# Attention ahead of two expert layers: its pieces in a listed order instead of a planned one

## The chip, the cores and the metric

The kernel runs on one core of one Trainium2 chip. The metric is the device time of one execution in microseconds (us), as the median of several executions. Engines are named as in the profile: PE (TensorE, matrix products), PEld (its loading of weights, which overlaps PE), DVE (VectorE), ACT (ScalarE), POOL (GpSimd) and SP (SyncE, which here issues DMA transfers). PSUM, where PE writes its products, has eight banks.

## What is computed

Attention in fp32 with 4 batches, 12 heads, 448 positions and head size 64, in which the heads are mixed before and after the softmax, and then two gated layers on the 1792 tokens of width 768:

```python
scores = scale * np.matmul(q, k.transpose(0, 1, 3, 2))
scores = np.einsum('bhij,hg->bgij', scores, w_pre)
scores = scores - np.max(scores, axis=-1, keepdims=True)
attn = np.exp(scores)
attn = attn / (np.sum(attn, axis=-1, keepdims=True) + 1e-09)
attn = np.einsum('bhij,hg->bgij', attn, w_post)
return np.matmul(attn, v)
...
x = (1 / (1 + np.exp(-(x @ w_gate))) * (x @ w_val)) @ w_out      # 768 -> 1536 -> 768
h = x @ w_in                                                      # 768 -> 2048
return (h * (1.0 / (1.0 + np.exp(-1.702 * h)))) @ w_out2          # -> 768
```

## The kernel before

The kernel first does the attention (function `attention`, L128) and then the layers (class `Ffn`). This change is about the attention, about 400 of 1308 us, and about the point at which one hands over to the other.

Each batch has four units of rows (three of 120, one of 88), 16 units in all, and each unit is cut into groups of rows that fill the 128 partitions with all heads, 92 groups `s` in all. PE's work comes in five kinds of pieces, called by a letter from here on:

- **T**, `turn` (L269): four transposes of q or k (some pieces have two), into one bank; ACT or DVE copies the high part out, DVE makes the low part.
- **S**, `qk` (L309): the scores of one pair of heads of one unit, six matmuls into two banks; two copies to `sc` by ACT or DVE (`qk_out`).
- **P**, `premix` (L337): the heads' first mixing for one group, from a tile `gt` that two DMAs (`relayout`, L328, issued by SP) fill out of `sc`. There are five `gt` tiles: group s can be moved when P of group s-5 is done. P writes two banks; then DVE takes the maxima (L343), ACT the exponentials (L349), ACT, DVE and POOL make the scaled second mixing matrix (L357, L359, L362).
- **O**, `postmix` (L384): the second mixing of the group, 56 short matmuls in the trace, into two banks; two copies to `at` by ACT or DVE (`post_out`).
- **A**, `av` (L405): the product with v for one unit, in two halves. Each half has three thirds of 16 matmuls, which write one bank.

T, S, P and O, and A divide PE's array in different ways ("rows", "quad" and "columns" in the code).

The order of all pieces on all engines is made by a planner when the kernel is built. `Work.add` (L37) takes a piece with its due time, its cost on each engine that can do it, what it needs, what buffers and how many banks it takes. `Work.order` (L60) then again and again takes the piece that can start first by these costs, picks its engine and its banks, and reckons a delay in PE's supply of instructions (`fetched`, L48, with blocks of 256). Every engine then does its pieces in that order, one behind the other; semaphores keep the dependences.

`add_scores` (L474) makes a piece of two pairs of heads for all units but the first, where it is one pair. `add_av` (L526) makes one piece of a whole half (`AVS` has one entry of three thirds), so an A piece is 48 matmuls. Beside this, `prepare` (L890) converts 28 blocks of the layers' weights during the attention, and `begin` (L794) adds the first steps of the layers: loads of x, the conversion of four blocks of weights, and 12 first pieces of matmuls (`early`, L831; written `pg` in the trace, six matmuls each). In these four blocks the storing of a converted block to memory (L869, by SP) belongs to the piece `conv3` on DVE, so it stands in SP's queue where `conv3` stands in the order.

Of the kernel before, what the change touches and what calls it, by code (L numbers as in the profile page):

```python
# [20 lines left out]
class Work:  # L21
# [20 lines left out]
                                load=load, lead=lead))  # L42
        return self.pieces[-1]

    def room(self, x):
        return sorted((t, b) for b, t in self.open.items() if b < self.kept or not x["late"])[:x["wants"]]

    def fetched(self, x, start):  # L48

        busy, late = x["engines"]["PE"]  # L50
        at, left, n = start, x["size"], self.room_in
        since = self.since
        while left > n:
            at += busy * n / x["size"]
            left -= n
            at = since = max(at, since + FETCH)
            n = BLOCK
        return at + busy * left / max(x["size"], 1) - start - busy, n - left, since

    def order(self):  # L60
        now = {}
        self.room_in, self.since = FIRST_BLOCK, -FETCH
        self.loaded = 0.0
        mode = None
        open_ = sorted(self.pieces, key=lambda x: (x["due"], x["i"]))
        done = []
        while open_:
            best = None
            for x in open_[:AHEAD] + open_[-FILL:]:
                if any(n["end"] is None for n in x["needs"] + x["behind"]):  # L70
                    continue
                at = max([n["end"] - x["lead"] for n in x["needs"]] + [n["begin"] for n in x["behind"]] + [x["since"]])
                wants = {p: x["takes"].count(p) for p in x["takes"]}
                if any(len(self.free[p]) < c for p, c in wants.items()):
                    continue
                at = max([at] + [sorted(self.free[p])[c - 1] for p, c in wants.items()])
                if x["wants"]:
                    room = self.room(x)
                    if len(room) < x["wants"]:
                        continue  # L80
                    at = max(at, room[-1][0])
                for e, (busy, _) in x["engines"].items():
                    start = max(at, now.get(e, 0.0))
                    key = (start + (self.fetched(x, start)[0] if x["size"] else 0.0), x["due"], x["i"])
                    if best is None or key < best[0]:
                        best = (key, x, e)
            _, x, e = best
            start = max([n["end"] - x["lead"] for n in x["needs"]] + [n["begin"] for n in x["behind"]] + [x["since"], now.get(e, 0.0)] +
                        [sorted(self.free[p])[x["takes"].count(p) - 1] for p in x["takes"]] + [t for t, _ in self.room(x)])
            busy, late = x["engines"][e]  # L90
            if e == "PE" and x["mode"] != mode:
                start += self.modes[mode == "quad"]
                mode = x["mode"]
            if x["size"]:
                wait, self.room_in, self.since = self.fetched(x, start)
                busy, late = busy + wait, late + wait
            if x["load"]:
                self.loaded = max(self.loaded, start + ISSUE) + x["load"]
                late += self.loaded - start
            for p in x["takes"]:  # L100
                self.free[p].remove(min(self.free[p]))
            x["banks"] = [b for _, b in self.room(x)]
            for b in x["banks"]:
                del self.open[b]
            x["begin"] = start
            x["end"] = start + late
            now[e] = start + busy
            for p in x["gives"]:
                self.free[p].append(x["end"])
            for y, n in x["frees"]:  # L110
                self.open[y["banks"][n]] = x["end"]
            open_.remove(x)
            done.append((start, x["i"], x, e))
        self.span = max(x["end"] for x in self.pieces)
        done.sort(key=lambda y: y[:2])
        return [(x, e) for _, _, x, e in done]


AHEAD = 400
BLOCK = 256  # L120
FIRST_BLOCK = 193
FETCH = 4090
ISSUE = 1451
END = 1e9
FILL = 140


def attention(tc, q, k, v, w_pre, w_post, xd, after):  # L128
# [8 lines left out]
    B, H, S, D = q.shape  # L137
    NP = H // 2
# [18 lines left out]
    for b in range(B):  # L157
        i0 = 0
# [22 lines left out]
    with ExitStack() as ctx:  # L181
# [243 lines left out]
        build_w()  # L425

        STEP = 3581
        AVS = ((0, 1, 2),)
        AVH = 3824
        AVR = 0  # L430
        TAIL = first[len(units) - 1]
# [94 lines left out]
        def add_av(u):  # L526
            b, i0, n = units[u]
            t = (first[u] + last[u] + 2) * STEP + -5918
            late = first[u] + last[u] + 1 >= TAIL
            prev = []  # L530
            x = None
            for half in range(2):
                for some in AVS:
                    done = half == 1 and some is AVS[-1]
                    y = work.add(t + half * AVH + some[0] * AVR, dict(PE=(21 * n - len(some) + 3, 21 * n + 180)),
                                 lambda e, half=half, some=some: av(u, half, some), needs=[] if x else out[u] + [vready[b, c] for c in range(2)],
                                 behind=[x] if x else [], banks=0 if some[0] else 1, late=late, mode="columns", size=32 * len(some),
                                 gives=() if not done else ("a", "v") if u % nu == nu - 1 else ("a",))
                    x = y
                    if some[0] == 0:  # L540
                        holds = x
                prev = [work.add(t + half * AVH + 2410, dict(ACT=(585, 840), DVE=(560, 720)), lambda e, half=half: av_out(u, half, e),
                                 needs=[x] + prev, takes=() if half else ("xo",), frees=((holds, 0),))]
                if not late:
                    in_banks.append(prev[0])
            stored[u] = work.add(t + 7200, dict(SP=(690, 500)), lambda e: store(u), needs=prev, gives=("xo",), load=1440)
# [5 lines left out]
        for b in range(B):  # L552
# [6 lines left out]
            for ci in range(nu):  # L559
                u = b * nu + ci  # L560
                span = last[u - 1] + 1 if u else 0
                for p in range(0, NP, 2):
                    if u:
                        add_scores(u, (p, p + 1), (first[u - 1] + 1.0 * p / NP) * STEP + 2604)
                    else:
                        for x in range(2):
                            add_scores(u, (p + x,), (p + x - 10) * STEP)
                for g in range(last[u] + 1):
                    add_group(first[u] + g)
                if ci == 0:  # L570
                    for c in range(2):
                        vready[b, c] = work.add((first[u] + 2 + 2 * c) * STEP + 1113, dict(SP=(800, 1000)), load=(2650, 2070)[c],
                                                emit=lambda e, b=b, c=c: load_v(b, c), takes=("v",) if c == 0 else (),
                                                behind=[vready[b, 0]] if c else [], since=0 if b else THIRD)
                add_av(u)
# [14 lines left out]
class Ffn:  # L590
# [203 lines left out]
    def begin(self, work, due, left, stored):  # L794
# [18 lines left out]
        for i in range(n):  # L813
            chain = [stages[i]]
            for j, (f, engines) in enumerate(((self.bits, dict(ACT=(920, 1140))), (self.conv1, dict(DVE=(270, 360))),
                                              (self.conv2, dict(DVE=(470, 560))), (self.conv3, dict(DVE=(470, 560))),
                                              (self.high, dict(ACT=(420, 530))), (self.low, dict(DVE=(470, 560))))):
                x = work.add(due + 10 * i + 2 + j, engines, lambda e, f=f, i=i: self.once(f, i), needs=chain[-1:],
                             takes=("wc",) if j == 0 else (), gives=((), (), (), ("wst",), (), ("wc",))[j],
                             behind=last if j == 4 else ())  # L820
                last = [x] if j == 4 else last
                chain.append(x)
            whole.append(chain[-1])
        prev = []
# [60 lines left out]
    def conv3(self, i):  # L885
        if self.units[i][0] == "f":
            self.steps[i][3]()
            self.steps.pop(i)[4]()

    def prepare(self, work, pf, pc):  # L890
# [111 lines left out]
    def split(self):  # L1002
# [2 lines left out]
        assert not self.held()  # L1005
        k = self.step
        self.step += 1
        for f, i in ((self.bits, k + 1), (self.conv2, k - 1), (self.conv1, k), (self.conv3, k - 1),
                     (self.high, k - 1), (self.low, k - 2), (self.sum, k)):
            self.once(f, i)  # L1010
        while (len(self.staged) < min(self.most, self.calm) and
# [730 lines left out]
```

## Time and profile before

| what | value |
|---|---|
| median of 3 runs | 1309.22 us (1305.79 to 1309.75) |
| the profiled execution, its time | 1309.51 us |
| the profiled execution, its span | 1307.8 us |
| PE busy in the span | 1260.1 us, 96% |
| DVE, ACT, POOL busy | 77%, 63%, 4% |
| first P starts | 24.31 us after the span's start |
| first matmul of the layers' second product (`pv`) | 411.59 us |

The span runs from the first to the last instruction; 1.7 us of the execution lie around it. A view by stages gives each engine's busy time in a stretch. The view of waits adds up the idle time of an engine ahead of its instructions, by what ended it; "issue" is idle time for which the profile shows no semaphore that ended it. The timeline merges equal instructions that follow each other, with the idle time ahead of them in brackets. PE's matmuls are pipelined and their ends are modelled, so the time that a piece of PE takes is read from its start to the start of the next piece.

### The profile page before, as it was taken

To read this page: it belongs to the slowest core of one execution; us is meant where nothing else is said; L and a number is where in the kernel's file an instruction comes from. 1 tells how busy PE (TensorE), PEld (TensorE's weight loads), DVE (VectorE), ACT (ScalarE), POOL (GpSimd) and SP (SyncE) were. 2 spreads that over 40 slices of the span, in tenths; PEclk is the share of its full clock that TensorE was granted. 3 is DMA by queue.
4 is the path that set the end of the run, shared out by engine and by line. 5 is a ranking of instruction groups with operands and counts; after the bars stand their busy time and mean duration, and the time that the engine had idled before them with its cause. 6 is when DMAs were issued, how large, how long until landed. Compare 5 with 4: busy or idle time off the path is not lost.

```text
span 1307.8 us, 33181 instructions
## 1 busy us (share of the span) xinstructions
PE 1260.1 (96%) x12770; PEld 1112.6 (85%) x12770; DVE 1007.0 (77%) x2147; ACT 819.6 (63%) x1963; POOL 50.2 (4%) x126
## 2 busy tenths in 40 slices
PE   8899899899999999999999999999999999999998
PEld 5677667667668989989998899999999989999998
DVE  7686688787776899889789898778865796565763
ACT  5677677787774667766666666555665465565432
POOL 3100010111110000000000000000000000000000
PEclk9999999999998999999999999999999999999999
DMA  6877867756766455578977445885715872125643
GB/s 180 214 211 228 219 200 224 216 163 190 227 218 235 158 168 178 174 258 302 307 245 275 138 148 164 287 281 188 247 56 169 288 267 86 49 61 155 209 153 121
DMA packets 224303, 256.87 MB, mean 196 GB/s; under 512 B 69628, under 2 KB 211600, under 8 KB 224144
## 3 DMA queue, kind: packets, MB, share of 16 engines
q1 hardware_dynamic: 218352, 253.35, 61.6%
q8 instruction: 101, 1.65, 0.5%
q10 hardware_dynamic: 5664, 1.38, 0.5%
q14 instruction: 58, 0.48, 0.1%
q0 software_dynamic: 128, 0.01, 0.0%
HBM read 160.18 MB, written 55.97 MB: 165 GB/s over the span
## 4 chain that ended last, share of the span: by engine, by line
PE 49%; DVE 6%; DMA 5%; ACT 2%; issue 2%; SPq 0%; DVEq 0%; ACTq 0%
PE pq L1123 28%; PE po L1610 15%; PE py L1068 6%; DMA ws<-in_moe_w_in_dram 3%; DMA sb<-xy 2%; DVE w L990 1%; DVE xy L1105 1%; DVE wc L865 1%; DVE wc L867 1%; DVE s L1261 1%; DVE s L1132 1%; ACT ws L862 0%; DMA wf<-sb 0%; ACT xy L1104 0%; DMA kept<-wc 0%
## 5 line engine op out<-in xcount | busy, mean ns | idle before, releaser
L1123 PE MATMUL pq<-xy,w 128*128 128x448 f32 x2394 | 483.1, 363 | 4.0 <-ACT s L1172 1.1
L1123 PEld LDWEIGHTS pq<-xy,w 128*128 128x128 f32 x2394 | 447.3, 187 | 39.0 <-ACT w L984 2.6
L1610 PE MATMUL po<-wf,xy 128*128 128x384 f32 x1176 | 206.9, 337 | 2.9 <-ACT xy L1056 1.6
L1610 PEld LDWEIGHTS po<-wf,xy 128*128 128x128 f32 x1176 | 206.0, 188 | 3.5 <-ACT xy L1056 1.8
L1068 PE MATMUL py<-xy,w 128*128 128x448 f32 x864 | 173.7, 362 | 1.4 <-DVE xy L1054 1.4
L1068 PEld LDWEIGHTS py<-xy,w 128*128 128x128 f32 x864 | 161.9, 187 | 12.9 <-DVE xy L1054 2.1
L384 PEld LDWEIGHTS bank<-w,ex 60*64 60x64 f32 (+1 forms) x5152 | 102.3, 136 | 41.0 <-issue 29.3
L349 ACT ACTIVATE ex<-bank,st 128x448 f32<-128x448 f32 x184 | 116.5, 639 | 30.4 <-DVE st L343 29.7
L343 DVE TENSOR_REDUCE st<-bank 128x1 f32<-128x448 f32 x184 | 106.8, 615 | 34.1 <-PE bank L337 33.1
L1104 ACT CAST xy<-xy 128x384 fp32r<-128x384 f32 (+2 forms) x212 | 89.2, 457 | 59.4 <-DVE xy L1261 56.5
L384 PE MATMUL bank<-w,ex 60*64 60x60 f32 (+2 forms) x5152 | 110.1, 222 | 15.5 <-issue 11.6
L337 PE MATMUL bank<-gt,wpre 64*64 64x448 f32 x736 | 109.2, 565 | 11.3 <-issue 5.4
L1105 DVE TENSOR_TENSOR xy<-xy 128x384 fp32r<-128x384 f32 (+2 forms) x212 | 95.7, 484 | 23.8 <-ACT xy L1104 23.7
L1261 DVE TENSOR_TENSOR xy<-xy 128x384 f32<-128x384 f32 (+2 forms) x184 | 90.7, 510 | 13.7 <-DMA xy<-kept 6.9
L984 ACT CAST w<-xy 128x384 fp32r<-128x384 f32 x110 | 55.1, 510 | 53.6 <-DVE xy L1261 32.1
L405 PEld LDWEIGHTS bank<-at,vt 128*64 128x64 f32 x1536 | 74.7, 139 | 12.0 <-ACT ex L349 4.4
L861 ACT ACTIVATE wc<-ws 128x384 f32<-128x384 f32 x108 | 59.8, 553 | 33.5 <-DMA ws<-in_moe_w_in_dram 22.9
L405 PE MATMUL bank<-at,vt 128*64 128x120 f32 (+1 forms) x1536 | 78.5, 262 | 1.4 <-issue 0.8
L990 DVE TENSOR_TENSOR w<-wt,w 128x384 fp32r<-128x384 f32 x108 | 59.1, 552 | 26.7 <-ACT w L984 26.7
L309 PE MATMUL bank<-kq 64*120 64x448 f32 (+1 forms) x576 | 73.5, 388 | 1.2 <-DVE kq L290 0.5
L1132 DVE TENSOR_TENSOR s<-s,pq 128x448 f32<-128x448 f32 x80 | 49.2, 616 | 28.4 <-PE pq L1123 28.4
L309 PEld LDWEIGHTS bank<-kq 64*120 64x120 f32 (+1 forms) x576 | 49.2, 178 | 23.1 <-issue 3.9
(97 smaller groups left out, 1530.1 us busy)
## 6 DMA issues: line engine op xcount, KB each, us to landing
gt<-sc SPq DMA_DIRECT2D x160, 210.0 KB
wf<-sb SPq DMA_DIRECT2D x64, 384.0 KB
xy<-kept SPq DMA_DIRECT2D x60, 384.0 KB
ws<-in_moe_w_out_dram SPq DMA_DIRECT2D x56, 384.0 KB
kept<-wc SPq DMA_DIRECT2D x108, 192.0 KB
ws<-kept SPq DMA_DIRECT2D x46, 384.0 KB
sb<-xy SPq DMA_DIRECT2D x32, 384.0 KB
ws<-in_moe_w_in_dram SPq DMA_DIRECT2D x32, 384.0 KB
```

The costliest lines, as they stand in the source:

```text
L309: nc.tensor.matmul(ps[a][:n, :S], w[at_, qp, 1, i0:i0 + n], w[at_, kp, 0], start=(i == 0), stop=(i == 2), tile_position=(a * 64, 0))
L337: nc.tensor.matmul(pre[s][row][64 * col:64 * col + 64, :S], wpre[r], x[r, col], start=True, stop=True, tile_position=(64 * row, 64 * col))
L343: nc.vector.tensor_reduce(out=rs[s][:, j:j + 1], in_=pre[s][j][:, :S], axis=AX.X, op=ALU.max, negate=True)
L349: nc.scalar.activation(ex[s][:, j], pre[s][j][:, :S], AF.Exp, bias=st[:, j:j + 1], scale=1.0, accum_out=st[:, 2 + j:3 + j])
L384: nc.tensor.matmul(ps[row][64 * k:64 * k + 64, c, :, j * m:(j + 1) * m], e[r, j, (c + k * NC) * 64:(c + k * NC + 1) * 64], w[r, j, :, i0:i ...
L405: nc.tensor.matmul(psv[u, half][a * 64:a * 64 + 64, r, :n], vt[:, g, c, :], at[:, c, g, :n], start=(c == 0), stop=(c == NC - 1), tile_posi ...
L1068: self.nc.tensor.matmul(acc[hb][:, :self.S], st, act[k0 + kc][hb][:, ap], start=(k0 + kc == 0 and part == 0 and ap == 0), stop=(k0 + kc == ...
L1104: self.nc.scalar.copy(dst[:, 0], src)
L1105: self.after(n, lambda: self.nc.vector.tensor_tensor(out=dst[:, 1], in0=src, in1=dst[:, 0].bitcast(F32), op=ALU.subtract))
L1123: nc.tensor.matmul(x, st, A[p][c][:, ap], start=(first and c + part + ap == 0), stop=(c == self.KG - 1 and part == 1), skip_group_check=no ...
L1261: self.nc.vector.tensor_tensor(out=dst, in0=x, in1=y, op=op)
L1610: nc.tensor.matmul(acc[:, :PW], x[:, part], w[:, wp], start=(start and part == 0 and wp == 0), stop=(stop and part == 1), skip_group_check ...
```

## The change

`Work.order` no longer plans. It reads a table, `PLAN`, of one token per piece (its number, in some tokens a letter for the engine, and after a colon the banks), asserts that needs, buffers and banks allow it, and returns that order. `add_scores` gets one pair of heads each time (96 pieces for 51), `AVS` has three entries of one third (96 pieces for 32), and the storing of the four early weights becomes the piece `keep` on SP. The pieces' instructions are the same ones; 2001 pieces become 2114. Cut to its core:

```diff
     def order(self):
-        now = {}
-        self.room_in, self.since = FIRST_BLOCK, -FETCH
...
-        open_ = sorted(self.pieces, key=lambda x: (x["due"], x["i"]))
         done = []
-        while open_:
-            best = None
-            for x in open_[:AHEAD] + open_[-FILL:]:
...
+        for token in PLAN.split():
+            number, _, banks = token.partition(":")
+            e = engines.get(number[-1])
+            x = self.pieces[int(number[:-1] if e else number, 36)]
...
+            x["banks"] = [int(b) for b in banks]
...
+PLAN = """
+0Y 3:0 1S 6:1 7V 8 cY f:2 oS 4V pS 5 gV 20:34 21V r:5 u:6 sV 10Y 1oY 1r:7 1pS 1u:1 dS i:0 1cY 11S vV t 2Y 1dS
...
-        AVS = ((0, 1, 2),)
+        AVS = ((0,), (1,), (2,))
...
-                    y = work.add(t + half * AVH + some[0] * AVR, dict(PE=(21 * n - len(some) + 3, 21 * n + 180)),
+                    y = work.add(t + half * AVH + some[0] * AVR, dict(PE=(7 * n * len(some), 7 * n * len(some) + 180)),
...
-                for p in range(0, NP, 2):
-                    if u:
-                        add_scores(u, (p, p + 1), (first[u - 1] + 1.0 * p / NP) * STEP + 2604)
-                    else:
-                        for x in range(2):
-                            add_scores(u, (p + x,), (p + x - 10) * STEP)
+                for p in range(NP):
+                    add_scores(u, (p,), ((first[u - 1] + 1.0 * p / NP) * STEP + 2604) if u else (p - 10) * STEP)
...
+                                              (self.keep, dict(SP=(500, 900))),
...
     def conv3(self, i):
         if self.units[i][0] == "f":
             self.steps[i][3]()
+
+    def keep(self, i):
+        if self.units[i][0] == "f":
             self.steps.pop(i)[4]()
```

Nearly all rows of the attention stand in another place. Behind the hand-over nothing moves: on PE all rows from `pv` on are the same, on DVE the last 1313 rows, on ACT the last 1054, on SP the last 522.

The first place is PE just behind the first P. `bank<-gt,wpre` is P (four rows), `bank<-ident,nat` T and `bank<-kq` S. Before:

```order
L337 MATMUL bank_259<-gt_274,wpre 64x448
L337 MATMUL bank_255<-gt_274,wpre 64x448
L337 MATMUL bank_259<-gt_274,wpre 64x448
L337 MATMUL bank_255<-gt_274,wpre 64x448
L269 MATMUL bank_251<-ident,nat 128x112 x4
L337 MATMUL bank_263<-gt_275,wpre 64x448
L337 MATMUL bank_267<-gt_275,wpre 64x448
L337 MATMUL bank_263<-gt_275,wpre 64x448
L337 MATMUL bank_267<-gt_275,wpre 64x448
L269 MATMUL bank_271<-ident,nat 128x112 x4
L337 MATMUL bank_243<-gt_276,wpre 64x448
L337 MATMUL bank_247<-gt_276,wpre 64x448
```

Now:

```order
L367 MATMUL bank_247<-gt_275,wpre 64x448
L367 MATMUL bank_259<-gt_275,wpre 64x448
L367 MATMUL bank_247<-gt_275,wpre 64x448
L367 MATMUL bank_259<-gt_275,wpre 64x448
L339 MATMUL bank_251<-kq 120x448
L339 MATMUL bank_271<-kq 120x448
L339 MATMUL bank_251<-kq 120x448
L339 MATMUL bank_271<-kq 120x448
L339 MATMUL bank_251<-kq 120x448
L339 MATMUL bank_271<-kq 120x448
L299 MATMUL bank_255<-ident,nat 128x112 x4
L367 MATMUL bank_263<-gt_276,wpre 64x448
```

The last S of unit 1 has moved from ahead of the first P to between the second and the third. Behind the rows shown, PE before has P, O, O, P, O, P and then two S; now it has P, O, P, O, P, S, P, O.

The second place is PE's end of the attention, behind the last O. `bank<-at,vt` is A (24 rows are half a unit) and `pg` the layers' first pieces. Before:

```order
L1068 MATMUL pg<-xy,w 128x448 x6
L405 MATMUL bank_251<-at,vt 64x88 x24
L405 MATMUL bank_255<-at,vt 64x88 x24
L1068 MATMUL pg<-xy,w 128x448 x24
L1068 MATMUL pv<-xy,w 128x448 x36
```

Now:

```order
L1099 MATMUL pg<-xy,w 128x448 x6
L435 MATMUL bank_247<-at,vt 64x88 x24
L435 MATMUL bank_243<-at,vt 64x88 x8
L1099 MATMUL pg<-xy,w 128x448 x6
L435 MATMUL bank_243<-at,vt 64x88 x8
L1099 MATMUL pg<-xy,w 128x448 x6
L435 MATMUL bank_243<-at,vt 64x88 x8
L1099 MATMUL pg<-xy,w 128x448 x12
```

The last two thirds of A now stand each behind a piece of the layers. Ahead of the rows shown, before has three O, a `pg` piece and two O; now four O in a row, a `pg` piece and one O.

## Rows read from the trace of the kernel before

**Rows 1.** Stages: length, busy us of each engine (instructions), granted clock, DMA share.

```profile
24.30:386.30 362.00, 335.87 (x7690) 245.89 (x7688) 276.10 (x588) 265.06 (x737) 37.53 (x91) 0.99 0.73 208
386.30:411.60 25.30, 21.64 (x425) 18.64 (x422) 17.55 (x37) 16.49 (x39) 0.53 (x1) 0.87 0.67 224
411.60:1307.80 896.20, 884.13 (x4543) 835.32 (x4541) 696.06 (x1479) 527.80 (x1166) 0.00 (x0) 1.00 0.58 192
```

**Rows 2.** Timeline of PE from 46 us: start, us, instruction; the five kinds of pieces.

```profile
46.86 0.98 PE L337 MATMUL bank<-gt,wpre 64*64 64x448 f32 x8
47.66 1.09 PE L384 MATMUL bank<-w,ex 60*64 60x60 f32 x56
48.69 1.48 PE L309 MATMUL bank<-kq 64*120 64x448 f32 x12
50.10 5.14 PE L405 MATMUL bank<-at,vt 128*64 128x120 f32 x96
55.17 0.98 PE L337 MATMUL bank<-gt,wpre 64*64 64x448 f32 x8
55.97 1.03 PE L384 MATMUL bank<-w,ex 60*64 60x60 f32 x54
56.80 0.59 PE L337 MATMUL bank<-gt,wpre 64*64 64x448 f32 x2
...
57.75 0.98 PE L269 MATMUL bank<-ident,nat 112*128 112x112 f32 x8
58.67 1.09 PE L384 MATMUL bank<-w,ex 60*64 60x60 f32 x54
```

**Rows 3.** Waits of PE's matmuls, 24.3 to 411.6 us: total us, times, longest.

```profile
PE bank L384 <- issue: 11.6, 11, 2.5
PE bank L337 <- issue: 5.4, 3, 3.8
PE bank L337 <- DMA gt<-sc: 3.5, 7, 0.9
```

**Rows 4.** DMA queues up to 411.6 us: the queue that brings instructions, packets and MB.

```profile
q8 instruction: 65, 1.06, 1.1%
```

**Rows 5.** Timeline of PE: the longest stall, PE behind it, and a short stall.

```profile
38.89 1.77 PE L337 MATMUL bank<-gt,wpre 64*64 64x448 f32 x8 [3.85 <-issue]
40.59 2.17 PE L309 MATMUL bank<-kq 64*120 64x448 f32 x12
...
371.94 0.69 PE L384 MATMUL bank<-w,ex 60*64 60x60 f32 x28 [0.52 <-issue]
```

**Rows 6.** Waits of PE's weight loads, 24.3 to 411.6 us.

```profile
PEld bank L337 <- DMA gt<-sc: 12.9, 17, 1.7
PEld bank L337 <- ACT ex L349: 7.3, 13, 1.9
PEld bank L384 <- POOL w L362: 5.0, 9, 1.0
...
PEld bank L337 <- ACT at L273: 3.1, 6, 1.3
```

**Rows 7.** Stretches at a lower clock; columns as in the stages.

```profile
38.89:43.60 4.71, 4.71 (x76) 2.82 (x78) 2.66 (x6) 1.96 (x7) 0.39 (x1) 0.66 0.81 182
143.80:148.10 4.30, 4.23 (x18) 1.23 (x20) 1.16 (x2) 0.94 (x5) 0.00 (x0) 0.60 0.78 230
328.40:332.40 4.00, 3.93 (x85) 3.65 (x87) 2.19 (x6) 1.18 (x3) 0.62 (x1) 0.57 0.84 168
396.00:406.70 10.70, 9.18 (x158) 8.26 (x157) 7.35 (x16) 5.44 (x13) 0.00 (x0) 0.68 0.32 117
```

**Rows 8.** Timeline of PE from 386 us: the end of the attention.

```profile
397.52 1.94 PE L384 MATMUL bank<-w,ex 60*64 60x48 f32 x55 [2.46 <-issue]
399.39 2.61 PE L1068 MATMUL pg<-xy,w 128*128 128x448 f32 x6
401.93 4.81 PE L405 MATMUL bank<-at,vt 128*64 128x88 f32 x96
```

## What the change was predicted to do

> **What bounds the kernel now.** I read the stages first [rows 1]. The attention ends at 411.6 us, where the layers' second product starts; the 896.2 us behind it keep PE busy for 884.1, and the change leaves their rows as they are on every engine. So I let these 896.2 us stand and forecast only the stretch ahead of 411.6. Between 24.3 and 386.3 us PE has work in 335.9 of 362 us, DVE in 276.1 and ACT in 265.1: DVE is at 76% and ACT at 73%, so PE is the engine that sets the pace there, and what counts is what PE waits for and how fast it runs.
>
> Second, what the pieces take when nothing disturbs them [rows 2], from one start to the next: P 0.80 us (46.86 to 47.66), O 0.83 (55.97 to 56.80) when another P follows and 1.03 (47.66 to 48.69) when S follows, two S 1.41, the six thirds of A 5.07, two T 0.92. I take P 0.80, O 0.90, S 0.70, a third of A 0.82 (0.61 in a unit of 88 rows, by its columns), T 0.44. From 24.3 to 411.6 us PE does 92 P, 92 O, 84 S, 96 thirds, 36 T and 37 matmuls of the layers at 0.2 us: 73.6 + 82.8 + 58.8 + 73.7 + 15.8 + 7.4 = 312 us. The stretch has 387.3. Some 75 us are more than the work, and that is the stock from which another order can take.
>
> Third, what they are. The matmuls' idle time that is put to no semaphore is the largest part, 11.6 + 5.4 = 17.0 us in 14 waits [rows 3]; the longest is 3.85 us [rows 5], the last of over 2 us is 2.46 [rows 8]. This is PE waiting for its own instructions: up to 411.6 us its queue brings 1.06 MB in 65 packets [rows 4], some 16 KB each, and PE's 16,465 matmuls and loads [rows 1], with some 235 semaphore instructions, make 256 for each packet; 12 of these 14 stalls begin at the same place in a block of 256. Then the `gt` tiles' DMAs: 12.9 us ahead of the weight loads of P [rows 6], 3.5 of which PE's matmuls show as idle [rows 3]. Then the softmax chain and the banks: 5.0 us of O on POOL, 7.3 of P on the exponentials, 3.1 of P on the copies to `at` [rows 6]. Then the clock: in four stretches the granted clock is 0.57 to 0.68, a mixture of 2.4 and 1.2 GHz, which costs 4.71 x 0.34 + 4.30 x 0.40 + 4.00 x 0.43 + 10.70 x 0.32 = 8.5 us [rows 7]; the first comes straight behind the stall of 3.85 us, and there P takes 40.59 - 38.89 = 1.70 us for 0.80 [rows 5]. The rest is changes between divisions of the array and small waits.
>
> **The change, part by part.** The instructions are the same, so the whole effect lies in distances on PE. I counted them in both orders by adding up the durations above, without any waiting, and set each threshold where the number of short distances before is near the number of waits of that kind.
>
> *`gt` tiles.* Group s can be moved when P of s-5 is done. Less than 8 us of PE's work lies between these two P 10 times before and twice now, of 87. Eight tenths of 12.9 us [rows 6] are 10.3; since waits overlap with others I take **-8**, with bounds of -3.5 (what PE's matmuls show [rows 3]) and -11.
>
> *Softmax chain.* Less than 5 us of work between P and O of one group: 12 times before (9 waits on POOL [rows 6]), 3 now. Three quarters of 5.0 us: -3.8. *Banks of O*: reused with under 0.9 us of work between, 18 times before and 4 now, of 178; four fifths of 3.1 us: -2.4. *Banks of P*: the first reused under 1.8 us or the second under 3.0, 21 times before, 20 now: nothing. The two gains will partly be covered by each other: **-4**, bounds -6 and +3 (if P's banks, 7.3 us for 13 waits, get as many more waits as there are more single S that take such banks).
>
> *Supply of instructions.* I cut both orders into blocks of 256 instructions (an O has 112 in 0.9 us, a P 16, a third of A 32) and summed the work in each. A block that starved took 4.2 us at the quickest, the one that ends with the stall at 371.94 us [rows 5]. Blocks with less than 4.1 us of work: 20 before, 28 now, and what they lack adds up to 13.5 and 19.1 us. The count for before lies under the measured 17.0. The ratio of 1.41 gives 24, +7. Against it, the block of the longest stall [rows 5] has 2.7 us of work before and 4.6 now, since a single S, T and P stand between the O; that takes some 2 of the 3.85 us. I take **+5**, bounds -6 and +10.
>
> The Trainium skill ("Runtime: NRT & Kernel Launch", Instruction fetch mechanics) says that crossing a 16 KiB boundary is mostly hidden. The 17.0 us of this trace say otherwise; by that rule this term would be 0 and the sum 5 us lower.
>
> *Clock.* Each of the four stretches stands behind a stall. The first stall should shrink below 2 us, and at the end single thirds of A now wait behind pieces of the layers where 4.81 us of A ran at the low clock [rows 8]. Of 8.5 us I take half: **-4**, bounds -8 and +5 (three more such stretches at 1.7).
>
> *Singles and thirds.* The division of the array changes 152 times for 136; a change out of P and O costs 1.03 - 0.90 = 0.13 us [rows 2]. 16 x 0.13 = **+2**. The cutting itself adds no instruction.
>
> The Trainium skill ("TensorEngine Tiling (Array Packing)", Key Properties) says that a change of the tiling mode drains TensorE, which speaks against more and smaller pieces; the 0.13 us per change are this trace's price for it.
>
> *Who copies, and `keep`.* ACT gets a net 3 copies more, DVE 3 fewer, at 0.5 to 0.7 us each; both have a fourth of their time free, and I cost it at nothing. `keep` takes four stores out of the rows behind `conv3` in SP's queue, where only the last unit's store and loads for later steps stand behind; nothing. If that cover is gone (the loads of x late), the layers' first pieces wait at the hand-over, about as long as PE's stall of 2.46 us there now [rows 8].
>
> Sum: -8 - 4 + 5 - 4 + 2 = -9. The profiled execution took 1309.5 us (span 1307.8 and 1.7 around it), as good as the median of 1309.2. The forecast is 1300.
>
> **The rivals.** *A larger gain.* All waits for `gt`, chain, O's banks and clock go (12.9 + 8.1 + 8.5) and the fetch gives neither more nor less: -29.5 + 2, **1282**. For it: the shortest distances rose in every kind but P's banks, and 75 us are there to take. Against it: a wait that goes shortens the block it stood in, and 28 blocks now lie under what a fetch takes.
>
> *The fetch takes it back.* What PE no longer waits for elsewhere it waits for at block ends: eight more short blocks at 17.0 / 14 = 1.2 us are +10, and of the gains -5, -4 and -3 remain, with +2: **1309**, no change. For it: 19.1 against 13.5 us; against it: the first long stall's block is mended.
>
> *Slower, by starved blocks and the clock.* Six blocks have under 2.8 us of work now, three before; three of the six lie at the end, where four O stand in a row. The price of one that starves in full is the 3.85 us of [rows 5] and 1.6 of slow clock behind it [rows 7]: 5.45. Before, the three cost some 7.8 us. All six in full: 32.7 - 7.8 - 15 (`gt`, chain and half the clock) + 2 = +12, **1321**. It decides from four of six on.
>
> *It does nothing.* If the queues of DVE and ACT really set the pace, distances on PE don't matter: **1309**. At 76% and 73% busy this is unlikely.
>
> **How the numbers follow.** Forecast (1294 to 1306) 0.40, larger gain 0.20, taken back 0.22, slower 0.13, nothing 0.05. About 0.3%, 4 us, is what can be told from no change here. Faster by more: 0.39 + 0.20 + 0.05 of the third case = 0.64. Within it: 0.01 + 0.12 + 0.05 = 0.18. Slower: 0.05 + 0.13 = 0.18. The range of 8 in 10 leaves out half of the larger gain and two thirds of the slower case: 1283 to 1315.
>
> **What would show it.** `pv` should start near 402 us for 411.6, with 896 us behind it unchanged; if that part moves, the premise is wrong. PE's issue waits should come to 20 to 24 us (17.0), weight loads waiting on `gt` to under 5 (12.9), O on POOL under 2 (5.0). At 39 us no stall of over 2 us should stand. There should be two or three stretches at the low clock, and none behind the four O at the end; if there is one with a stall of 3 us ahead of it, the slower case is at work. The forecast is wrong if the waits fall as counted and the stretch is as long as before, for then something that the distances on PE don't show sets the pace.

## The result and the profile after

| | before | after |
|---|---|---|
| median of 8 runs each, us | 1309.56 | 1295.53 |
| lowest to highest, us | 1305.79 to 1317.59 | 1290.69 to 1302.21 |
| ratio, 95% interval | | 0.9889 [0.9859, 0.9918] |
| the profiled execution, us | 1309.51 | 1302.21 |
| `pv` starts at, us | 411.59 | 406.13 |
| from `pv` to the end, us | 896.2 | 894.3 |

The changed kernel is 14.0 us faster; 9 were forecast, and 1295.5 lies inside the range. One caution goes with everything below: the profiled execution of after is the slowest of its eight runs, 6.7 us above their median, so its trace shows more waiting than a usual run has. In after's lines the attention's numbers are larger by 30: T is L299, S L339, P L367, O L414, A L435.

The stages of after, with the columns of [rows 1]:

```profile
26.20:381.00 354.80, 323.51 (x7670) 245.65 (x7670) 272.41 (x580) 264.92 (x744) 35.01 (x90) 0.97 0.73 212
381.00:406.10 25.10, 21.40 (x452) 18.78 (x448) 16.91 (x38) 16.56 (x39) 1.03 (x2) 0.93 0.59 187
406.10:1300.40 894.30, 884.69 (x4543) 837.44 (x4542) 698.29 (x1485) 528.05 (x1167) 0.00 (x0) 1.00 0.59 193
```

The last row is that of [rows 1] again, 894.3 for 896.2 us: the part behind the hand-over stood still, and the gain lies ahead of it. The first two rows of both traces, added up, say where: PE's busy time fell from 357.5 to 344.9 us, and its idle time rose from 29.8 to 35.0. In this trace, then, the gain is not in the gaps between matmuls. The waits of PE's weight loads for semaphores (all rows of the view of [rows 6] except issue) fell from 60.5 to 37.2 us, and part of such a wait lies inside PE's busy time: of the longest one for `gt` in before, 1.7 us [rows 6], only 0.90 shows as idle (the row at 285.42 further down). What PE's matmuls wait for, 24.3 to 406.2 us (answers to [rows 3]; total us, times, longest):

```profile
PE bank L414 <- issue: 28.5, 16, 5.3
PE bank L339 <- issue: 2.0, 1, 2.0
PE bank L339 <- ACT ex L379: 1.4, 4, 0.8
PE bank L435 <- ACT ex L379: 0.9, 1, 0.9
```

And its weight loads (answers to [rows 6]):

```profile
PEld bank L414 <- POOL w L392: 3.1, 8, 0.8
...
PEld bank L367 <- ACT at L303: 1.0, 2, 0.6
PEld bank L367 <- ACT ex L379: 1.0, 3, 0.5
PEld bank L367 <- DMA gt<-sc: 0.9, 1, 0.9
```

P hardly waits any more: for `gt` 0.9 us (12.9 before), for the exponentials 1.0 (7.3), for the copies to `at` 1.0 (3.1). What has grown is "issue": 28.5 + 2.0 + 0.5 = 31.0 us, where before has 17.8, the 17.0 of [rows 3] and another 0.8 on A. The longest of it, in PE's timeline of after:

```profile
226.74 0.38 PE L414 MATMUL bank<-w,ex 60*64 60x60 f32 x6 [0.75 <-issue]
...
230.20 0.91 PE L414 MATMUL bank<-w,ex 60*64 60x60 f32 x44
236.41 2.41 PE L414 MATMUL bank<-w,ex 60*64 60x60 f32 x68 [5.30 <-issue]
238.75 2.60 PE L339 MATMUL bank<-kq 64*120 64x448 f32 x12
```

An O stops after 44 of its 56 matmuls (the next row of 68 is its last 12 and another O), PE stands for 5.30 us, and the two S behind take 2.60 us, where the pair in [rows 2] takes 1.48: a stall and then a lower clock, the pattern of [rows 5].

### The profile page after: what moved, and what is told of

It is laid out like the page before. It is cut to its first block, busy times and chain, and to the rows that moved or that the text cites. A ratio compares the mean times of both kernels' runs of the same rounds, so it can differ in the third digit from the quotient of the medians.

```text
span 1300.4 us, 33168 instructions
## 1 busy us (share of the span) xinstructions
PE 1249.1 (96%) x12770; PEld 1115.4 (86%) x12770; DVE 1006.5 (77%) x2147; ACT 816.7 (63%) x1963; POOL 48.2 (4%) x126
## 4 chain that ended last, share of the span: by engine, by line
PE 53%; DVE 7%; DMA 2%; issue 1%; ACT 1%; SPq 0%; DVEq 0%; ACTq 0%
PE pq L1154 27%; PE po L1641 14%; PE py L1099 12%; DVE xy L1136 2%; DVE w L1021 1%; DVE xy L1292 1%; DMA xy<-kept 1%; DVE s L1292 1%; DMA sb<-xy 1%; DVE wc L893 1%; DVE s L1163 1%; DMA wf<-sb 0%; ACT xy L1135 0%; DVE wc L892 0%; DVE wc L895 0%
## 5 line engine op out<-in xcount | busy, mean ns | idle before, releaser
L1099 PEld LDWEIGHTS py<-xy,w 128*128 128x128 f32 x864 | 161.9, 187 | 12.9 <-DVE xy L1085 2.1
L414 PEld LDWEIGHTS bank<-w,ex 60*64 60x64 f32 (+1 forms) x5152 | 101.1, 138 | 52.4 <-issue 45.9
L414 PE MATMUL bank<-w,ex 60*64 60x60 f32 (+2 forms) x5152 | 106.0, 224 | 29.0 <-issue 28.5
L1136 DVE TENSOR_TENSOR xy<-xy 128x384 fp32r<-128x384 f32 (+2 forms) x212 | 95.8, 486 | 24.4 <-ACT xy L1135 24.3
L367 PE MATMUL bank<-gt,wpre 64*64 64x448 f32 x736 | 90.0, 557 | 0.6 <-DMA pf<-in_moe_w_gate_dram 0.5
L435 PEld LDWEIGHTS bank<-at,vt 128*64 128x64 f32 x1536 | 74.0, 137 | 12.9 <-ACT ex L379 3.9
L339 PE MATMUL bank<-kq 64*120 64x448 f32 (+1 forms) x576 | 77.7, 401 | 4.8 <-issue 2.0
L435 PE MATMUL bank<-at,vt 128*64 128x120 f32 (+1 forms) x1536 | 79.1, 261 | 1.5 <-ACT ex L379 0.9
L303 ACT COPY at<-bank 128x480 f32<-128x480 f32 (+1 forms) x105 | 55.5, 564 | 39.3 <-PE bank L414 39.1
L889 ACT ACTIVATE wc<-ws 128x384 f32<-128x384 f32 x108 | 59.8, 554 | 29.8 <-DMA ws<-in_moe_w_in_dram 20.1
L339 PEld LDWEIGHTS bank<-kq 64*120 64x120 f32 (+1 forms) x576 | 52.0, 185 | 25.8 <-ACT ex L379 5.3
```

The lines of the kernel that those rows point to most:

```text
L339: nc.tensor.matmul(ps[a][:n, :S], w[at_, qp, 1, i0:i0 + n], w[at_, kp, 0], start=(i == 0), stop=(i == 2), tile_position=(a * 64, 0))
L367: nc.tensor.matmul(pre[s][row][64 * col:64 * col + 64, :S], wpre[r], x[r, col], start=True, stop=True, tile_position=(64 * row, 64 * col))
L414: nc.tensor.matmul(ps[row][64 * k:64 * k + 64, c, :, j * m:(j + 1) * m], e[r, j, (c + k * NC) * 64:(c + k * NC + 1) * 64], w[r, j, :, i0:i ...
L435: nc.tensor.matmul(psv[u, half][a * 64:a * 64 + 64, r, :n], vt[:, g, c, :], at[:, c, g, :n], start=(c == 0), stop=(c == NC - 1), tile_posi ...
L1099: self.nc.tensor.matmul(acc[hb][:, :self.S], st, act[k0 + kc][hb][:, ap], start=(k0 + kc == 0 and part == 0 and ap == 0), stop=(k0 + kc == ...
L1136: self.after(n, lambda: self.nc.vector.tensor_tensor(out=dst[:, 1], in0=src, in1=dst[:, 0].bitcast(F32), op=ALU.subtract))
```

## Experiments

Ratios are to before's runs of the same call, with 95% intervals. `pv`, waits and clock are of one profiled execution each. "Clock" is what the stretches below full clock cost ahead of `pv`: the length of each, as the trace's record of the granted clock has it, times the share of the clock that it lacks, 8.5 us before and 11.9 after. Idle time inside such a stretch is counted too, so the figure is an upper bound.

### Cutting without the list

The planner of before, with single pairs, thirds and `keep`.

```diff
-        AVS = ((0, 1, 2),)
+        AVS = ((0,), (1,), (2,))
...
-                for p in range(0, NP, 2):
...
+                for p in range(NP):
+                    add_scores(u, (p,), ((first[u - 1] + 1.0 * p / NP) * STEP + 2604) if u else (p - 10) * STEP)
```

> Before's planner orders the pieces, but the pieces are cut as in the changed kernel (single pairs, thirds, keep apart); no listed order. Theory (the gain is from where the listed order puts pieces on PE): no gain from the cutting, 1305 to 1315 us. Rival (smaller pieces are what helps): near the changed kernel, 1292 to 1300 us.

Measured: 1312.73 us, ratio 1.0029 [1.0005, 1.0053]; `pv` at 414.13. Waits of PE's matmuls up to there:

```profile
PE bank L384 <- issue: 6.8, 5, 2.8
PE bank L384 <- ACT sc L273: 4.7, 2, 2.4
PE bank L384 <- ACT ex L349: 4.3, 7, 2.2
PE bank L384 <- POOL w L362: 2.1, 3, 0.8
```

The finer pieces alone bring nothing. The planner did with them much of what the list does for `gt` (4.9 us of weight loads' waiting, 12.9 before) and better than the list for issue (6.8 us), and paid with O waiting behind softmax and score copies, on ACT and POOL. The gain is in what the list sets (places, and with them engines and banks), not in the cutting.

### The thirds of A put back together

After's list, with the three thirds of each half moved to the place of the last.

```diff
+            if after and x["third"] < 2:
...
+                done.insert(m, moved)
```

> The changed kernel, with the thirds of each half of A put back side by side (each at the place of its last third); the list is else the same. Theory: the cutting into thirds is worth little in this list, 1294 to 1301 us. Rival (the thirds fill gaps that nothing else fills): over 1302 us.

Measured: 1295.96 us, ratio 0.9884 [0.9818, 0.995], as after. Thirds are worth nothing that these four runs can show. This trace (1298.26 us) also shows an execution with less waiting in nearly the same order: `pv` at 400.96, issue 24.3 us, clock 8.5.

### `keep` back inside `conv3`

```diff
     def conv3(self, i):
         if self.units[i][0] == "f":
             self.steps[i][3]()
+            self.steps.pop(i)[4]()
...
     def keep(self, i):
-        if self.units[i][0] == "f":
-            self.steps.pop(i)[4]()
+        pass
```

> The changed kernel, with the storing of the four early weights put back into the piece that makes them (the listed place of the store does nothing). Theory: 0, 1292 to 1299 us. Rival (the hand-over gains from the store's own place): 2 to 5 us slower.

Measured: 1298.07 us, ratio 0.9917 [0.9885, 0.9949], beside after's 0.9889 [0.9859, 0.9918]: the intervals overlap, so `keep` is worth something between nothing and a few us. PE's timeline at the hand-over shows one wait that after has not:

```profile
395.77 2.65 PE L1099 MATMUL pg<-xy,w 128*128 128x448 f32 x6 [4.15 <-ACT w L1015]
```

Against that, `pv` came at 403.19, ahead of after's profiled 406.13. This stays open.

### A sixth `gt` tile in before

The prediction let a group's move wait for P of s-5, that is for a free tile. Here before's order, row for row, gets six tiles for five (for room, one `xo` tile for two).

```diff
-    PF = 4
+    PF = 5
...
-        xo_p = ctx.enter_context(tc.tile_pool(name="xo", bufs=2))
+        xo_p = ctx.enter_context(tc.tile_pool(name="xo", bufs=1))
```

> The order of the kernel before, frozen as a list, with a sixth gt tile (and one xo tile for two, to make room): group s can be moved when P of group s-6 is done, and nothing else moves. Theory (the short distances between P of s-5 and P of s were worth some 8 us): the weight loads' wait for gt falls from 12.9 us to under 6 and the time to 1300 to 1305 us. Rival (P waits for the transfer itself, or for something else at the same moment): 1306 to 1312 us.

Measured: 1311.14 us, ratio 1.0015 [0.9987, 1.0044], and the weight loads of P wait as before:

```profile
PEld bank L390 <- DMA gt<-sc: 15.3, 18, 2.1
```

So tiles were not what P waited for; the expected 1300 to 1305 us did not come. One of the 17 waits of before shows what it did wait for. SP's timeline of before, and PE's:

```profile
276.25 4.28 SPq L328 DMA_DIRECT2D gt<-sc  x4
```

```profile
273.87 1.45 PE L309 MATMUL bank<-kq 64*88 64x448 f32 x12
...
285.42 0.97 PE L337 MATMUL bank<-gt,wpre 64*64 64x448 f32 x4 [0.90 <-DMA gt<-sc]
```

The unit's last two S run until 275.25. Then their copies end and SP issues the moves, one after the other; those of the group whose second half waits at 285.42 go out at 278.02 and 278.90, while P of s-5 had ended at 260.35. Two of the 17 waits have no s-5; in the other 15 the tile had been free for 2.3 us or more when the first move was issued. P waited for a transfer that had been issued only shortly before: from the start of the last move's issue to the end of the wait lie 3.7 to 6.5 us at 13 of the 17, and 8.0 to 10.7 at the other four (144.73, 146.33, 237.57 and 339.34), where halves of v had been issued just before. Moves of a unit wait for the copies of its last S, and from the end of that S to the start of the unit's first P lie 9.2 us in the median before and 15.0 after. From the start of the last move's issue to P lie less than 4.5 us 15 times of 92 before, once after. The list widened both distances, from P of s-5 and from the last S. The sixth tile shows that the first was not the cause; that the second was is argued, since no run changes it alone.

### The loads of v left out, in both orders

SP's timeline of after ahead of the stall of 5.30 us:

```profile
222.29 1.67 SPq L358 DMA_DIRECT2D gt<-sc  x2
224.06 0.48 SPq L931 DMA_DIRECT2D pf<-in_moe_w_val_dram  x1
224.65 1.69 SPq L325 DMA_DIRECT2D vt<-in_v_dram  x2
226.39 0.84 SPq L358 DMA_DIRECT2D gt<-sc  x1
```

Both halves of v for the next batch (768 and 576 KB) are issued back to back from 224.65 on, and at 226.74 PE passes from one block of 256 instructions to the next. In before 3.8 us, a store and a `gt` move lie between the two halves. DMA queues of after from there on, first 226.70 to 233.50, then 233.50 to 236.50 us (packets, MB, share):

```profile
q1 hardware_dynamic: 1649, 1.49, 107.3%
```

```profile
q1 hardware_dynamic: 260, 0.30, 45.3%
q8 instruction: 1, 0.02, 2.8%
```

For 6.8 us the engines move bulk data alone; then the instruction packet comes through, at 233.61, and PE goes on at 236.41. The list issues the halves back to back for the last batch too (318.57 and 319.29), and a stall of 3.81 us ends at 329.41. For the second batch they go out 3.9 us apart (132.05 and 135.93), and the largest stall in the 20 us behind is 1.16. To test it, v is loaded for the first batch only:

```diff
+            if b:
+                return
             nc.sync.dma_start(vt[64 * x:64 * x + 64, :, :c.stop - c.start],
```

> The changed kernel, but v is loaded for the first batch alone; the loads of the other three batches (1.34 MB each) are left out, so these batches multiply with the first one's v. PE's order is untouched. Theory (an instruction block comes late because its fetch stands behind a bulk transfer that was issued just before): the stalls of 1.2, 5.3 and 3.8 us behind these loads shrink to under 1 us each and the slow clock behind them goes, 1281 to 1289 us. Rival (a stall is set by how many instructions stand in a block alone): stalls and time as in the changed kernel, 1293 to 1299 us.

> The kernel before, with v loaded for the first batch alone; the loads of the other three batches are left out, so these multiply with the first one's v. Theory (fetches of instructions stand behind bulk transfers in the kernel before too): of its 17 us of issue waits those behind the loads at 129, 225 and 318 us go, some 7 us, and the slow clock at 328 us with them: 1295 to 1302 us, less than the 21 us that the same edit took from the changed kernel. Rival (only the changed order is sensitive): 1306 to 1312 us.

Measured: after's order 1274.33 us, ratio 0.9737 [0.9703, 0.977], under the expected 1281 to 1289; before's 1297.4, ratio 0.9894 [0.9859, 0.9929]. The loads cost 21 us with the list and 12 with the plan. Without them the list is worth 1297.4 - 1274.3 = 23 us, with them 14. Waits without the loads, first of after's order, then of before's:

```profile
PE bank L416 <- issue: 6.6, 8, 1.7
...
PE bank L341 <- issue: 0.9, 1, 0.9
```

```profile
PE bank L386 <- issue: 7.3, 9, 1.7
PE bank L339 <- issue: 5.2, 2, 4.1
```

After's order then waits less for instructions than before's (8.2 us with a last 0.7 on A, against 12.5), though it has 28 blocks with under 4.1 us of work against 20. The number of short blocks is not what decides. Clock: 1.7 and 6.8 us. Not all of the fall from 31.0 to 8.2 us is due to the loads: up to 132 us this run has after's rows and loads, and there three block ends that stall 2.15, 2.40 and 0.99 us in after's trace stall 0, 0.36 and 0.72 in this one.

### The loads of v issued twice

```diff
+            nc.sync.dma_start(vt[64 * x:64 * x + 64, :, :c.stop - c.start],
+                              v[b].rearrange("h (m g) d -> m h g d", g=HC)[:, :, c])
```

> The changed kernel, with every load of v issued twice (the same bytes to the same tile). Theory (fetch behind bulk): another 1.34 MB ahead of the fetch in each batch, some 6 us of delay at each of four places, less what other blocks hide: 1303 to 1318 us. Rival (it was the place and not the bytes): 1293 to 1300 us.

Measured: 1335.78 us, ratio 1.018 [1.0133, 1.0228], above the expected range; `pv` at 440.83. This run does not test what it was made for. The two issues of a half are not queued one behind the other: the second waits in SP's queue until the first has landed, and the moves to `gt` and the loads of k stand behind it. SP's waits for the loads of v, then what PE's matmuls wait for:

```profile
SPq L327 <- DMA vt<-in_v_dram: 62.6, 8, 8.9
```

```profile
PE bank L416 <- issue: 22.1, 13, 3.8
PE bank L369 <- DMA gt<-sc: 12.6, 4, 6.9
PE bank L437 <- issue: 8.7, 3, 7.7
PE bank L299 <- DMA nat<-in_k_dram: 6.3, 1, 6.3
```

The 7.7 us on A are hardly a wait for instructions either. SP's timeline, then PE's:

```profile
262.06 0.60 SPq L327 DMA_DIRECT2D vt<-in_v_dram  x1
```

```profile
268.40 7.23 PE L437 MATMUL bank<-at,vt 128*64 128x120 f32 x96 [7.67 <-issue]
```

A reads v, whose last half was issued 6.3 us ahead, and this wait begins at place 14 of a block of 256 instructions, all others that are put to issue here at 193 or 194 (see the last experiment). At the block ends PE waits 25.5 us, less than after's 31.0. The loads cost 40 us more when issued twice, but these are waits for late transfers (12.6 + 6.3 + 7.7 us) and the clock (25.6 us for 11.9). That more bytes make the wait for instructions longer is not shown.

### The loads of v cut

After, with each of the two loads of a batch in three transfers of four heads, one behind each of SP's following pieces; the bytes are the same.

```diff
+            for h in range(0, H, 4):
+                hs = slice(h, h + 4)
+                parts.append(lambda hs=hs: nc.sync.dma_start(
...
+            if parts and e == "SP":
+                parts.popleft()()
```

> The changed kernel, with each load of v cut into six transfers (192 to 256 KB) that are issued one after each following piece of SP. Theory (fetch behind bulk): the stalls at the loads of v get shorter, 1285 to 1293 us. Rival (the same bytes delay the fetch as long, or density alone sets the stall): 1293 to 1299 us.

> The changed kernel, with each load of v cut into twelve transfers (96 to 128 KB), one after each following piece of SP, where the cut into six took 6 us off the changed kernel. Theory (a fetch waits as long as the bytes that were queued just before it): 1282 to 1290 us. Rival (six pieces were enough, or SP's own time for twelve issues costs more): 1290 to 1296 us.

Measured: six transfers a batch 1289.56 us, ratio 0.9847 [0.9814, 0.988]; twelve (two heads each) 1290.58, ratio 0.9852 [0.9822, 0.9882], where 1282 to 1290 was expected. Six is the best version here that computes all of the reference, 6 us under after; the intervals of the two overlap by 0.002, and finer transfers give no more. In the six's trace `pv` starts at 389.21, issue is 19.3 us, clock 5.1, and what the later loads cost is small:

```profile
PE bank L420 <- issue: 17.6, 14, 2.9
...
PE bank L441 <- DMA vt<-in_v_dram: 0.9, 2, 0.6
```

In the twelve's trace issue is lower still, 14.1 us, but A waits 3.7 us for v. The two block ends behind the back-to-back halves, in every trace of after's order but that of the doubled loads (us of stall; before 1.53 and 2.33):

| | first, at 236 us in after | second, at 329 us in after |
|---|---|---|
| after | 5.30 | 3.81 |
| whole A | 4.75 | 4.09 |
| `keep` in `conv3` | 4.53 | 4.21 |
| 80 instructions later (below) | 5.63 | 4.62 |
| v cut in six | 1.20 | 0.22 |
| v cut in twelve | 0.41 | none |
| v's later loads left out | none | none |

Four traces with the loads as they are agree, and every kernel that cuts or drops them loses most of both stalls. This, more than the totals, shows the cause of these two.

### The same list, 80 instructions later in the blocks

40 tiny transposes, 80 PE instructions, ahead of the attention move every piece against the block ends.

```diff
+        for _ in range(40):
+            nc.tensor.transpose(bank[0][:32, :32], ident[:32, :32], ident[:32, :32])
```

> The changed kernel, with 40 small transposes of the identity on PE ahead of the first work, while PE waits for its first load: 80 instructions more, so that every piece of the attention lies 80 instructions later in the blocks of 256. Theory (an idle time that no semaphore ended is the wait for a block): the stalls begin at the same places in the blocks as before and so in other pieces; the count of short blocks is nearly the same (18.7 against 19.1 us), so 1291 to 1301 us. Rival (these waits belong to the pieces themselves): the stalls stay with their pieces and move by 80 in the blocks.

Measured: 1299.35 us, ratio 0.9925 [0.9893, 0.9956]. Cut PE's instructions, its semaphore instructions included, into blocks of 256 from the first that the trace has. Stalls of over 0.4 us that are put to issue then start at place 193 or 194 in all 16 cases of after and in all 15 here, though every piece lies 80 instructions later, so partly in other pieces. The first longer one, in PE's timeline of this kernel, then of after:

```profile
46.58 0.46 PE L414 MATMUL bank<-w,ex 60*64 60x60 f32 x12 [1.85 <-issue]
```

```profile
43.48 0.76 PE L414 MATMUL bank<-w,ex 60*64 60x60 f32 x18 [2.15 <-issue]
```

So these places are the ends of the blocks in which PE gets its instructions [rows 4], and there the fetch is paid. Moving them redistributes the stalls and does not remove them: issue is 28.2 us here too (26.0 on O, 1.5 on S, 0.7 on P).

## Why the prediction was right, and where it was not

**The premise and the sign held.** The part behind `pv` moved by 1.9 us, no more than between traces in which its rows are the same (892.3 with the sixth tile, 897.7 with v's loads cut), and the gain lies ahead of it. The rival "it does nothing" falls.

**`gt` tiles, -8: the waits went as forecast, the cause was wrong.** The waits fell from 12.9 to 0.9 us of weight loads, and to nothing at the matmuls, the forecast's under 5. But the step that counted P(s-5) to P(s) named the wrong releaser: a sixth tile changed nothing. The count matched because in the list that distance and the one from the last S to the first P grew together. What the term is worth in time was not measured by itself. A match of 10 short distances with 17 waits is no evidence on its own; the issue times of the moves, in the same trace, would have shown that the tile had long been free.

**Chain and banks, -4: about right.** O on POOL went from 5.0 to 3.1 us (under 2 was forecast), P on `at` 3.1 to 1.0, P on the exponentials 7.3 to 1.0, which I had held unchanged. But a good part of that moved: over all kinds of pieces the weight loads' waits on exponentials fell only from 15.6 to 12.7 us, since S and A wait for them now. The effect of this term alone was not measured.

**Supply of instructions, +5: right sign, too small, and the reason was wrong.** The only trace of after has 31.0 us for 17.8, which is +13 and above the bound of +10; two kernels close to it have 24.3 (whole A) and 22.6 (the store in `conv3`), where 20 to 24 was forecast. The step that turned short blocks into stalls failed: 28 short blocks wait 8.2 us when v's loads are gone. At the two largest stalls, what decides is what else the DMA engines are given just before a block ends: there the list put the two halves of v side by side. The loads of v cost about 9 us more with the list than with the plan (21 against 12); that the side-by-side halves are all of this is argued. So a part of the rival "the fetch takes it back" came true, by another mechanism. The Trainium skill ("Runtime: NRT & Kernel Launch", Instruction fetch mechanics) says that such a crossing is mostly hidden: by count the trace of after agrees (16 stalls of over 0.4 us at some 60 block ends), by cost it does not (31.0 us).

**Clock, -4: wrong.** 8.5 us became 11.9 (8.5 in the trace with whole A). Two of after's five stretches, with the columns of [rows 7]:

```profile
43.48:47.00 3.52, 3.52 (x32) 2.64 (x32) 0.10 (x1) 1.90 (x5) 0.00 (x0) 0.53 0.77 166
...
388.60:392.00 3.40, 3.40 (x108) 3.31 (x103) 0.73 (x2) 1.91 (x5) 0.00 (x0) 0.52 1.05 255
```

The granted clock of 0.53 and 0.52 lies near 1.2 of 2.4 GHz. Each of the five stands behind a stall of 1.95 us or more (not each such stall has one: behind 3.25 us at 311.79 the clock stayed full). So this term follows the longer standstills of PE, and as most of these are waits for instructions, it should not have been given the opposite sign to the supply term. Other waits do it too: in before, the stretch at 143.80 [rows 7] stands behind a wait for the exponentials.

```profile
143.87 4.20 PE L337 MATMUL bank<-gt,wpre 64*64 64x448 f32 x16 [1.83 <-ACT ex L349]
```

With v's later loads gone the term is 1.7 us, with all of them issued twice 25.6.

**The sum: near, in part by luck.** The two profiled executions lie 7.3 us apart. Supply took 13 us and the clock 3.4, where the forecast had +5 and -4, so everything else together gave some 24 us where the forecast had 10 (-8 - 4 + 2). The errors offset each other. This trace shows the gain in PE's busy time, which the terms reach only through the waits of the weight loads.

**The tail.** The mechanism of the slower rival did occur, at its own place and at less than its price. PE's timeline of after at the hand-over, the answer to [rows 8]:

```profile
388.30 3.56 PE L414 MATMUL bank<-w,ex 60*64 60x60 f32 x111 [2.45 <-issue]
391.79 1.50 PE L1099 MATMUL pg<-xy,w 128*128 128x448 f32 x6
...
396.73 2.65 PE L435 MATMUL bank<-at,vt 128*64 128x88 f32 x64
```

The four O stall for 2.45 us at their middle, and the two behind the stall run at the low clock, against the forecast that no such stretch would stand there; but A runs at full clock again, 2.65 us for 64 matmuls where [rows 8] have 4.81 for 96. The stall of 3.85 us at 38.89 [rows 5] became one of 2.15 at 43.48: it is the end of the same block (PE's instruction 707 in the trace before, 705 now), the one for which the forecast counted 2.7 us of work before and 4.6 now. It shrank by 1.7 us where some 2 were forecast, and stayed just over the 2 us named as the sign.

**The spread.** Eight runs of after lie 11.5 us apart, and 6.7 separate its trace from its median. The same rows do stall differently from one execution to the next: 2.15, 2.40 and 0.99 us against 0, 0.36 and 0.72 at the three block ends named above. That this is the cause of the spread, and that it depends on what the DMA engines happen to hold, is argued, not shown.

## What to carry to other kernels

Before costing an order by a free buffer, look up when the transfer into it was issued: if that is right behind its producer, the distance to widen is producer to consumer, and another buffer does nothing. Where an engine waits for its own instructions, look at which transfers were queued in the microseconds before, and cut and spread a large load that has time, rather than count instructions per block. Before a run is read as a test of more bytes, look whether the added transfer waits for the first: issued twice into one tile, it held up SP's queue instead. An order that takes waits away raises the share of those that remain, so weigh the move of each large DMA issue with as much care as that of the matmuls.

## What was new about the hardware

PE's instruction packet found no way past bulk data at the longest stall: in 6.8 us 1.49 MB of bulk moved and no instruction packet, and a stall of 5.30 us stood behind 1.34 MB of loads. Taking three quarters of those loads away gained 21 us, and cutting each into three transfers gave back 6 in the median and shortened this stall to 1.20 us. Stalls began at one place in the blocks of 256 instructions, 193 or 194 by the trace's count, whatever piece stood there.
